# A linear-attention and gated feed-forward kernel: how the stores of the later pairs' x are cut into rows

## The chip, the cores and the metric

The kernel runs on one core of one Trainium2 chip. The metric is device time in microseconds (us) of one execution. A core has a matrix engine (TensorE, PE in the rows; PEld is its loading of weights), a vector engine (VectorE, DVE), a scalar engine (ScalarE, ACT), GpSimd (POOL) and SyncE (SP), which issues nearly all DMAs here. The profile counts 16 DMA engines.

## What is computed

Sizes: 8 batches, 8 heads, 576 positions, 64 features a head; phi maps 64 features to 128 and takes both signs, 256 in all. The attention's output is x, 4,608 tokens of 512 features, and goes through a gated feed-forward net.

```python
def phi(x):
    proj = np.einsum('bhsd,df->bhsf', x, w_phi)
    proj = proj - np.max(np.abs(proj), axis=-1, keepdims=True)
    return np.concatenate([np.exp(proj), np.exp(-proj)], axis=-1)
q_p, k_p = (phi(q), phi(k))
kv = np.einsum('bhsf,bhsd->bhfd', k_p, v)
z = np.sum(k_p, axis=2)
num = np.einsum('bhsf,bhfd->bhsd', q_p, kv)
den = np.einsum('bhsf,bhf->bhs', q_p, z)[..., None] + 1e-06
x = (num / den).transpose(0, 2, 1, 3).reshape(B * S, H * D)
g = x @ w_gate
out = (g / (1 + np.exp(-g)) * (x @ w_val)) @ w_out
```

## The kernel before

The attention works on 32 pairs of heads (8 batches, 4 pairs each). Pairs 0 to 11 take one path (`finish_early`), pairs 12 to 31 another (`finish`); the change is in the second. The feed-forward net takes x in 12 chunks of 384 tokens, with x lying feature by feature (128 rows of features, tokens along the row). The first four chunks are computed plainly; the later eight in pairs of chunks, with sums of operands that save products (`operands`, `strassen`, line 1218). Each such pair of chunks is followed by the second layer (`rest`, line 388, products with `w_hi`, `hh` and the tiles `m`). Weights, their low parts, and the hidden layer pass through DRAM and are streamed in again: `stream_*<-wv_dram` and `tb<-wv_dram` (line 1152), `m<-h_dram` (line 994).

Since x of batches 2 and later is finished long before the net reads it, it goes through DRAM too, in `x_dram`, shaped [batch, 128 rows, 2 halves of the sequence, 4 pairs, 288 positions]. A pair has two heads of 64 features, and so 128 rows. In `finish`, a pair's normalised result lies in `num` with 128 partitions = (head h, half of the sequence u, position s of 32) and, along the row, nine blocks of 64 features. VectorE turns it in blocks of 32 by 32 (line 786): one instruction for each half g of the features, into `turned` with partitions (h, u, feature j of 32) and 288 positions along the row. Two pairs share the tiles (index r). After the second of them SP issues four stores (line 798), one for each h and g: 64 partitions (u, j), each with a row of 2 x 288 float32 numbers, 2,304 bytes. There are 20 such pairs, 10 groups of four stores. `turned` takes the place of `shared`, four tiles that the weights' conversion used earlier, and has two halves n used in turn, each filled again only when the stores of the pair before last are out (`last["sent", ...]`).

Before a pair of chunks is computed, `operands` loads x from `x_dram` into `stage` (line 1166), ACT rounds it into `tb` (line 1176) and VectorE takes the remainder (line 1177).

What is issued when is set by a planner (`Plan`): every step has an engine, a cost in ns and the steps that it waits for, and a run through these costs gives the order of each engine's queue. A transposition costs `dve(n)` = 150 + 1.04 n there, a DMA its bytes at 320 per ns and 2,400 ns. Where TensorE has nothing ready, the planner puts in filler matmuls (`idle`, lines 1415 and 1417). Each engine then works in order; SP's DMAs go round eight completion semaphores, so that each waits for the one eight places before it (the brackets in the order below).

Of the kernel before, what the change touches and what calls it, by code (L numbers as in the profile page):

```python
# [9 lines left out]
F32 = mybir.dt.float32  # L10
F32R = mybir.dt.float32r
U32 = mybir.dt.uint32
# [5 lines left out]
P = 128  # L18
S = 576
SH = S // 2  # L20
NBL = S // 32
D = 64
NF = 128
CH = 384
DM = 512
# [19 lines left out]
LATE_BATCH = 2  # L45
# [32 lines left out]
class Plan:  # L78
# [21 lines left out]
    def add(self, eng, cost, fn, after=(), rank=0.0, take=None, give=None, mode="whole"):  # L100
        port = eng in ("DVE2", "POOL")
        eng = eng[:3] if eng == "DVE2" else eng
        s = Step(eng, cost, fn, rank, len(self.steps), self.LAG[eng], take, give, (rank, len(self.steps)))
        s.port = port
        s.slack = self.SLACK.get(eng, 0) if 16 <= rank < 1000 and cost > 1 else 0
        s.mode = mode if eng == "PE" and cost > 1 else None
        seen = set()
        for a in after:
            if a is not None and id(a) not in seen:
                seen.add(id(a))  # L110
                a.then.append(s)
                s.left += 1
        self.steps.append(s)
        return s
# [146 lines left out]
def dve(n):  # L261
    return 150 + 1.04 * n
# [23 lines left out]
def favor_attention_moe(ctx: ExitStack, tc: tile.TileContext, qT, kT, v, w_phi, wg, wv, wo, out):  # L286
    nc = tc.nc
# [3 lines left out]
    pool = ctx.enter_context(tc.tile_pool(name="sb", bufs=1))  # L291
# [4 lines left out]
    x_dram = tc.dram_tile([NB - LATE_BATCH, P, 2, NK, SH], F32, name="x_dram")  # L296
# [36 lines left out]
    osb = sb("osb", [P, DM], F32, 2)  # L333


    shared = [pool.tile([P, 2 * DM], dt, name=f"shared{i}", tag=f"shared{i}") for i, dt in enumerate((U32, U32, F32, F32))]
    raw = [t.rearrange("p (n t) -> p n t", t=2) for t in shared[:2]]
    we, wa = ([t[:, i * DM:(i + 1) * DM] for i in range(2)] for t in shared[2:])
    late = {}
# [1 line left out]
    def later(name, tag, shape, dtype=F32R):  # L341
        if name not in late:
            late[name] = pool.tile(shape, dtype, name=name, tag=tag)
        return late[name]
# [22 lines left out]
    add = plan.add  # L367
# [111 lines left out]
            at = end  # L479
        return got  # L480

    turned_tiles = []

    def turned_tile(n, g):
        if not turned_tiles:
            turned_tiles.extend(pool.tile([P, 2, SH], F32, name=f"turned{m}", tag=f"shared{m}") for m in range(4))
        return turned_tiles[2 * n + g]

    STAGE_TAGS = ("xh1", "xl1")

# [27 lines left out]
    last = {}  # L518

    def attention(i, rank):  # L520
        b, pr = divmod(i, NPAIR)
        early = i < EARLY_PAIRS
        j = i % 2
        jq = j if early else 0
        vec = nc.vector
# [13 lines left out]
        n = 4 * P * P  # L539
# [11 lines left out]
        for g, (t0, t1) in enumerate(K_GROUPS):  # L551
# [4 lines left out]
            n = m2 * NF  # L556
# [19 lines left out]
            m = km[(3 * i + g) % len(km)]  # L576
# [67 lines left out]
        if early:  # L644
            for g in range(3):
                tail = g == 2
                w = 1 if tail else 4
                n = 3 * i + g
                key, key2 = ("q", i, g), ("t", i, g)
                m, y = km[n % len(km)], qy[n % 2]  # L650
# [103 lines left out]
        def finish(extra):  # L754
            features = lambda k, h, c: (qe, qx)[k][j][:, h, c]
            main, blocks_ = 7, NBL // 2
            slot_at = lambda n: (work[plan.bank["n", i, n // main]], n % main * VD)

            def over():
                for n in range(blocks_):  # L760
                    o, at = slot_at(n)
                    for k in range(2):
                        for h, r in enumerate(sides):
                            nc.tensor.matmul(o[r, at:at + VD], features(k, h, slice(D * n, D * n + D)),  # L764
                                             kvs[j][:, (2 * k + h) * VD:(2 * k + h + 1) * VD],
                                             start=n % main == 0 and k == 0, stop=n in (main - 1, blocks_ - 1) and k == 1)

            nu = add("PE", 2 * blocks_ * KV_PACE, over, [*f1, *kvc, *extra], rank,
                     take=[("n", i, 0), ("n", i, 1)], mode="columns")
            last["kvs", i] = last["nu", i] = last["qe", i] = last["qx", i] = nu  # L770
            parts_ = ((0, 0, main), (1, main, blocks_ - main))
            slots = lambda part, m: work[plan.bank["n", i, part]][:, :m * VD].rearrange("p (n d) -> p n d", d=VD)
            free = [*last.get(("num", i - 1), ()), last.get(("turned", i - 1))]
            dn = [add("ACT", 200, lambda part=part, at=at, m=m: nc.scalar.activation(
                den[:, at:at + m], slots(part, m)[:, :, D], AF.Copy, bias=1e-6), [nu, last.get(("rc", i - 1))], rank)
                for part, at, m in parts_]
            t1 = add("DVE", 200, lambda: vec.reciprocal(rc[:, :blocks_], den[:, :blocks_]), [*dn, *free], rank)
            last["rc", i] = t1
            even = num.rearrange("p (n d) -> p n d", d=D)
            normal = [add("DVE", dve(m * D), lambda part=part, at=at, m=m: vec.tensor_tensor(  # L780
                out=even[:, at:at + m], in0=slots(part, m)[:, :, :D], op=ALU.mult,
                in1=rc[:, at:at + m].rearrange("p (n o) -> p n o", o=1).broadcast_to([P, m, D])), [t1, *free], rank, give=("n", i, part))
                for part, at, m in parts_]
            n, r = i // 2 % 2, i % 2
            over_ = [*raw_free, *wa_free, *we_free] if i < EARLY_PAIRS + 4 else last["sent", i - r - 4]
            t3 = [add("DVE", dve(SH), lambda g=g: vec.transpose(
                turned_tile(n, g)[:, r].rearrange("p (n s) -> p n s", s=32), even[:, :, 32 * g:32 * g + 32]),
                [*normal, *over_], rank) for g in range(2)]
            last["turned", i] = t3[1]
            last["num", i] = t3  # L790
            if r == 0:
                last["half", i] = t3
                return
            t3 = [*t3, *last["half", i - 1]]
            sent = []
            for h in range(2):
                for g in range(2):
                    sent.append(add("SP", D * S * 4, lambda h=h, g=g: nc.sync.dma_start(
                        x_dram[b - LATE_BATCH, (2 * h + g) * 32:(2 * h + g + 1) * 32, :, pr - 1:pr + 1].rearrange("j p r s -> p j (r s)"),
                        turned_tile(n, g)[h * D:(h + 1) * D].rearrange("p r s -> p (r s)")), t3, rank))  # L800
            last["sent", i - 1] = sent
            for c, *_ in cuts:
                x_kept.setdefault(c, []).extend(sent)
# [69 lines left out]
        if early:  # L873
            finish_early([])
        elif i < DEFER:
            finish([])
        else:
            late_sums.append(finish)
# [70 lines left out]
    def first(c, f, low, held):  # L949

        n, lo, lo_ready = low
        a_hi, a_lo = xh[c % X_SETS], xl[c % X_SETS]
        ends = [None, None]
        order = [(a, k) for ks in ((0, 1, 2), (3,)) for a in range(2) for k in ks] if f == 0 else \
            [(a, k) for a in range(2) for k in range(NK)]
        count = [0, 0]
        for a, k in order:
            begin, final = count[a] == 0, count[a] == NK - 1
            count[a] += 1

            def go(a=a, k=k, begin=begin, final=final):
                begun.append(1)
                o = ps(("gv", a, held), CH)
                hi = w1_hi(f)
                matmuls([(o, hi[:, a, k], a_hi[:, k], begin, False), (o, hi[:, a, k], a_lo[:, k], False, False),
                         (o, lo[a][:, k], a_hi[:, k], False, final)])

            wait = list(lo_ready) + (x_ready[c, k] if f == 0 else [])
            if begin:
                wait.append(gv_read[a])  # L970
            ends[a] = product(3 * pe(CH), go, wait)
        lo_user[0][n].append(ends[1])
        if f == NFT - 1:
            x_free[c] = [ends[0], ends[1]]
        j = new_th()

        s1 = into(j, add("ACT", act(CH), lambda: nc.scalar.activation(th(j), ps(("gv", 0, held), CH), AF.Tanh, scale=0.5),
                         [ends[0]], FIRST))
        s2 = add("DVE", dve(CH), lambda: nc.vector.scalar_tensor_tensor(
            out=th(j), in0=th(j), scalar=1.0, in1=ps(("gv", 0, held), CH), op0=ALU.add, op1=ALU.mult), [s1], FIRST)  # L980
        gv_read[0] = s2
        s3 = add("DVE", dve(CH), lambda: nc.vector.tensor_tensor(out=th(j), in0=th(j), in1=ps(("gv", 1, held), CH), op=ALU.mult),
                 [s2, ends[1]], FIRST)
        gv_read[1] = s3
        return j, s3
# [378 lines left out]
    for f in range(NFT):  # L1364
# [3 lines left out]
        for c in range(EARLY):  # L1368
            j, h = first(c, f, low, 0)
# [18 lines left out]
    for f in range(NFT):  # L1388
        j, h = first(PLAIN - 1, f, low_parts(f, 0), 0)
# [80 lines left out]
```

## Time and profile before

| | us |
|---|---|
| median of 3 runs | 1231.64 (1229.57 to 1232.07) |
| the profiled execution | 1231.18 |
| its span, first to last instruction | 1229.4 |
| TensorE busy | 1172.2 (95%) |
| VectorE busy | 793.4 (65%) |
| ScalarE busy | 545.3 (44%) |
| GpSimd busy | 140.9 (11%) |
| mean granted TensorE clock | 0.978 of full speed |

298.32 MB move in 219,744 packets of the queue that SP fills, 243 GB/s as a mean; their time is 75.4% of what 16 DMA engines have. Engines' busy times overlap, so they say nothing yet of what the kernel waits for: that is read from stretches of the span, from the idle time of TensorE in them, and from what ended it. A granted clock of 1.00 is 2.4 GHz, 0.50 is 1.2 GHz.

### The profile page before, as it was taken

To read this page: it belongs to the slowest core of one execution; us is meant where nothing else is said; L and a number is where in the kernel's file an instruction comes from. 1 tells how busy PE (TensorE), PEld (TensorE's weight loads), DVE (VectorE), ACT (ScalarE), POOL (GpSimd) and SP (SyncE) were. 2 spreads that over 40 slices of the span, in tenths; PEclk is the share of its full clock that TensorE was granted. 3 is DMA by queue.
4 is the path that set the end of the run, shared out by engine and by line. 5 is a ranking of instruction groups with operands and counts; after the bars stand their busy time and mean duration, and the time that the engine had idled before them with its cause. 6 is when DMAs were issued, how large, how long until landed. Compare 5 with 4: busy or idle time off the path is not lost. (4 is left out here: it accounts for less than half of the span.)

```text
span 1229.4 us, 26393 instructions
## 1 busy us (share of the span) xinstructions
PE 1172.2 (95%) x9978; PEld 1026.6 (84%) x9978; DVE 793.4 (65%) x1593; ACT 545.3 (44%) x1233; POOL 140.9 (11%) x142
## 2 busy tenths in 40 slices
PE   9999999999999889998979899997999999799998
PEld 7777889999888768987967789896699897599986
DVE  7998899997567637676756255785345785434441
ACT  6887543333435435453534243553333553333332
POOL 1323200000132212010100001110001110001100
PEclk9999999999999989998989899998999999899999
DMA  5656778777999779986766688866688767779864
GB/s 162 175 162 186 247 249 288 249 254 234 333 310 303 253 253 339 344 240 201 242 189 184 198 283 285 241 211 212 221 270 286 238 213 221 244 233 309 281 200 160
DMA packets 220031, 298.32 MB, mean 243 GB/s; under 512 B 65280, under 2 KB 125824, under 8 KB 219904
## 3 DMA queue, kind: packets, MB, share of 16 engines
q1 hardware_dynamic: 219744, 296.56, 75.4%
q8 instruction: 79, 1.29, 0.5%
q14 instruction: 48, 0.39, 0.1%
q10 hardware_dynamic: 160, 0.07, 0.0%
HBM read 217.91 MB, written 78.64 MB: 241 GB/s over the span
## 5 line engine op out<-in xcount | busy, mean ns | idle before, releaser
L388 PE MATMUL work<-w_hi,hh 128*128 128x512 f32 x468 | 187.7, 409 | 24.6 <-ACT hh L1006 16.7
L381 DVE TENSOR_TENSOR m<-m,hh 128x384 fp32r<-128x384 f32 x132 | 74.8, 573 | 140.1 <-ACT hh L1006 122.1
L388 PE MATMUL work<-w_hi,m 128*128 128x512 f32 x396 | 160.6, 405 | 0.9 <-DVE m L381 0.9
L1240 DVE TENSOR_TENSOR m<-m,work 128x384 f32<-128x384 f32 x144 | 78.5, 552 | 121.9 <-ACT m L1237 73.2
L1006 ACT CAST hh<-m 128x384 fp32r<-128x384 f32 x144 | 73.1, 512 | 182.8 <-DMA m<-h_dram 92.3
L381 POOL TENSOR_TENSOR m<-m,m 128x384 f32<-128x384 f32 x48 | 58.4, 1216 | 646.3 <-DVE m L1245 365.3
L388 PE MATMUL work<-xh,w_big 128*128 128x384 f32 x384 | 132.3, 345 | 0.0
L388 PEld LDWEIGHTS work<-w_hi,hh 128*128 128x128 f32 x468 | 90.4, 193 | 48.0 <-ACT hh L1006 18.6
L388 PE MATMUL work<-xl,w_big 128*128 128x384 f32 x384 | 128.6, 335 | 0.0
L1218 PE MATMUL work<-tb,stream_xh 128*128 128x384 f32 x618 | 115.3, 338 | 0.0
L1218 PEld LDWEIGHTS work<-tb,stream_xh 128*128 128x128 f32 x618 | 107.0, 188 | 4.7 <-issue 3.8
L1237 ACT COPY m<-work 128x384 f32<-128x384 f32 x144 | 68.1, 474 | 79.2 <-PE work L1218 71.5
L1218 PE MATMUL work<-tb,stream_xl 128*128 128x384 f32 x468 | 90.8, 343 | 9.1 <-ACT m L1237 9.1
L1244 ACT ACTIVATE m<-m 128x384 f32<-128x384 f32 x96 | 45.4, 517 | 111.4 <-DVE m L1240 111.3
L388 PEld LDWEIGHTS work<-w_hi,m 128*128 128x128 f32 x396 | 76.5, 193 | 20.5 <-DVE m L381 2.4
L1218 PEld LDWEIGHTS work<-tb,stream_xl 128*128 128x128 f32 x468 | 82.7, 191 | 12.7 <-ACT m L1237 9.5
L588 ACT ACTIVATE kp<-kp 128x512 f32<-128x512 f32 x128 | 78.2, 630 | 24.4 <-DVE kp L583 23.2
L1218 PE MATMUL work<-tb,tb 128*128 128x384 f32 x408 | 79.3, 341 | 4.6 <-ACT m L1237 4.6
L388 PEld LDWEIGHTS work<-xh,w_big 128*128 128x128 f32 x384 | 72.2, 188 | 7.7 <-issue 4.8
L1218 PEld LDWEIGHTS work<-tb,tb 128*128 128x128 f32 x408 | 71.8, 191 | 7.5 <-ACT m L1237 4.9
L381 POOL TENSOR_TENSOR s<-s 128x256 f32<-128x256 f32 x48 | 43.1, 897 | 282.4 <-DMA s<-w_dram 250.4
L388 PE MATMUL work<-w_lo,hh 128*128 128x512 f32 x183 | 74.1, 405 | 0.0
(141 smaller groups left out, 2345.8 us busy)
## 6 DMA issues: line engine op xcount, KB each, us to landing
stream_xh<-wv_dram SPq DMA_DIRECT2D x103, 256.0 KB
h_dram<-m SPq DMA_DIRECT2D x124, 192.0 KB
m<-h_dram SPq DMA_DIRECT2D x124, 192.0 KB
stream_xl<-wv_dram SPq DMA_DIRECT2D x78, 256.0 KB
tb<-wv_dram SPq DMA_DIRECT2D x77, 256.0 KB
w_lo<-wlo_dram SPq DMA_DIRECT2D x72, 256.0 KB
stream_w_lo<-wv_dram SPq DMA_DIRECT2D x52, 256.0 KB
stream_xl<-wlo_dram SPq DMA_DIRECT2D x48, 256.0 KB
```

What stands on the lines that cost most here:

```text
L381: (nc.gpsimd if on == "POOL" else nc.vector).tensor_tensor(out=o, in0=a, in1=b, op=op)
L388: nc.tensor.matmul(o, l, r, start=a, stop=z)
L588: nc.scalar.activation(kpv[:, :m2, s], kpv[:, :m2, 1], AF.Exp, scale=-1.0 if s else 1.0)
L1006: s4 = add("ACT", act(CH), lambda: nc.scalar.copy(hh[b], th(j)), [made, hid_free[b]], FIRST)
L1218: nc.tensor.matmul(o(), l, r, start=begin and k + m == 0, stop=k + m == 3, skip_group_check=True)
L1237: return j, into(j, add("ACT", act(CH), lambda: nc.scalar.copy(th(j), src()), after, FIRST))
L1240: return add("DVE", dve(CH), lambda: vec.tensor_tensor(out=th(j), in0=th(j), in1=src(), op=ALU.add), after, FIRST)
L1244: s1 = into(t, add("ACT", act(CH), lambda: nc.scalar.activation(th(t), th(j), AF.Tanh, scale=0.5), [ready], FIRST))
```

## The change

One tile `shared` of 4 x 1,024 numbers a row takes the place of four; `turned` becomes one tile [128, n, g, r, 288] in its place. A pair is turned by one VectorE instruction for both halves of the features instead of two. The four stores of two pairs are cut by head h and half of the sequence p instead of by h and g: each takes 32 partitions (feature j), and from each of them two rows of 2,304 bytes, one for each g. The outermost dimension, on both sides, is 32 where it was 2 in DRAM and 64 in SBUF. Bytes, the number of stores and the length of the rows stay.

```diff
-    shared = [pool.tile([P, 2 * DM], dt, name=f"shared{i}", tag=f"shared{i}") for i, dt in enumerate((U32, U32, F32, F32))]
+    shared = pool.tile([P, 4, 2 * DM], F32, name="shared", tag="shared")
+    shared = [shared[:, i].bitcast(dt) for i, dt in enumerate((U32, U32, F32, F32))]
...
-    turned_tiles = []
-
-    def turned_tile(n, g):
-        if not turned_tiles:
-            turned_tiles.extend(pool.tile([P, 2, SH], F32, name=f"turned{m}", tag=f"shared{m}") for m in range(4))
-        return turned_tiles[2 * n + g]
+    turned = lambda n: later("turned", "shared", [P, 2, 2, 2, SH], F32)[:, n]
...
-            t3 = [add("DVE", dve(SH), lambda g=g: vec.transpose(
-                turned_tile(n, g)[:, r].rearrange("p (n s) -> p n s", s=32), even[:, :, 32 * g:32 * g + 32]),
-                [*normal, *over_], rank) for g in range(2)]
-            last["turned", i] = t3[1]
+            t3 = [add("DVE", dve(S), lambda: vec.transpose(
+                turned(n)[:, :, r].rearrange("p g (n s) -> p n g s", s=32), even.rearrange("p n (g s) -> p n g s", g=2)),
+                [*normal, *over_], rank)]
+            last["turned", i] = t3[0]
...
             for h in range(2):
-                for g in range(2):
-                    sent.append(add("SP", D * S * 4, lambda h=h, g=g: nc.sync.dma_start(
-                        x_dram[b - LATE_BATCH, (2 * h + g) * 32:(2 * h + g + 1) * 32, :, pr - 1:pr + 1].rearrange("j p r s -> p j (r s)"),
-                        turned_tile(n, g)[h * D:(h + 1) * D].rearrange("p r s -> p (r s)")), t3, rank))
+                for p in range(2):
+                    sent.append(add("SP", D * S * 4, lambda h=h, p=p: nc.sync.dma_start(
+                        x_dram[b - LATE_BATCH, h * D:(h + 1) * D, p, pr - 1:pr + 1].rearrange("(g j) r s -> j g (r s)", g=2),
+                        turned(n)[(2 * h + p) * 32:(2 * h + p + 1) * 32].rearrange("p g r s -> p g (r s)")), t3, rank))
```

The planner's cost for a pair's transposition falls from 2 x 449.5 to 749 ns, and with it some of the order moves. Line numbers after the change are 4 lower behind the stores. First SP's queue about its first group of stores (`wv_dram<-s`, `s<-w_dram`: sums of weights; `vf`, `vl`, `kin`, `qin`: inputs of a pair; brackets: what it waits for), before and after:

```order
L1103 DMA wv_dram<-s_3532 128x2x256 [waits DMAHW2_49,Activation_49]
L994 DMA m_4596<-h_dram 128x384 [waits DMAHW3_49]
L989 DMA h_dram<-m_4594 128x384 [waits DMAHW4_49,DVE_49]
L798 DMA x_dram<-turned_4107 2x32x576 [waits DMAHW5_49]
L798 DMA x_dram<-turned_4108 2x32x576 [waits DMAHW6_49,DVE_49]
L798 DMA x_dram<-turned_4107 2x32x576 [waits DMAHW7_49]
L798 DMA x_dram<-turned_4108 2x32x576 [waits DMAHW0_49]
L932 DMA w_lo_89<-wlo_dram 128x512 [waits DMAHW1_49,PE_49]
L1106 DMA wv_dram<-s_3531 128x4x256 [waits DMAHW2_49,DVE_49]
```

```order
L990 DMA m_4361<-h_dram 128x384 [waits DMAHW0_49]
L532 DMA qin<-in_qT_dram 128x576 [waits DMAHW1_49,PE_49]
L794 DMA x_dram<-turned 32x2x576 [waits DMAHW2_49,DVE_49]
L794 DMA x_dram<-turned 32x2x576 [waits DMAHW3_49]
L794 DMA x_dram<-turned 32x2x576 [waits DMAHW4_49]
L794 DMA x_dram<-turned 32x2x576 [waits DMAHW5_49]
L525 DMA kin<-in_kT_dram 128x512 [waits DMAHW6_49,PE_49]
L529 DMA kin<-in_kT_dram 64x2x64 [waits DMAHW7_49,PE_49]
L940 DMA w_lo_85<-wlo_dram 128x512 [waits DMAHW0_49]
```

The group now stands 27 places earlier, ahead of the keys (`kin`) that it followed. Next VectorE where the third late pair is turned (`rc`, `num`: its normalisation), before and after:

```order
L777 RECIPROCAL rc<-den 128x9
L780 TENSOR_TENSOR num<-work_132,rc 128x448
L780 TENSOR_TENSOR num<-work_136,rc 128x128
L786 STREAM_TRANSPOSE turned_4109<-num 128x288
L786 STREAM_TRANSPOSE turned_4110<-num 128x288
L381 TENSOR_TENSOR m_4596<-m_4596,hh_122 128x384
```

```order
L776 TENSOR_TENSOR num<-work_129,rc 128x448
L776 TENSOR_TENSOR num<-work_130,rc 128x128
L782 STREAM_TRANSPOSE turned<-num 128x9x2x32
L382 TENSOR_TENSOR m_4579<-m_4579,hh_122 128x384
L382 TENSOR_TENSOR s_3528<-s_3528 128x256 x2
```

Two instructions became one of twice the length. Last TensorE at the start of the second layer behind the first pair of later chunks, where the number of filler matmuls changes, before and after:

```order
L388 MATMUL work_130<-w_hi_83,m_6777 128x512
L1417 MATMUL work_135<-idle 128x256 x3
L388 MATMUL work_135<-w_hi_84,hh_121 128x512
L388 MATMUL work_135<-stream_xl_5366,hh_121 128x512
L388 MATMUL work_135<-w_hi_84,m_6849 128x512
```

```order
L389 MATMUL work_127<-w_hi_73,hh_122 128x512
L389 MATMUL work_127<-stream_xl_5356,hh_122 128x512
L389 MATMUL work_127<-w_hi_73,m_6797 128x512
L1413 MATMUL work_132<-idle 128x256 x10
L389 MATMUL work_132<-w_hi_74,hh_123 128x512
L389 MATMUL work_132<-stream_xl_5356,hh_123 128x512
```

The three fillers ahead of the second hidden tile became one, and ten stand now ahead of the fourth; over the whole program those of line 1417 (1413 now) go from 60 to 67.

## Rows read from the trace of the kernel before

**Rows 1.** Busy us (instructions) by engine, clock, DMA share, GB/s; nine stretches and all:
```profile
core 0: us, PE busy (x) PEld busy (x) DVE busy (x) ACT busy (x) POOL busy (x), PEclk, DMA share, GB/s
410.70:450.70 40.00, 30.50 (x321) 25.17 (x318) 16.72 (x37) 11.97 (x28) 5.36 (x7) 0.88 0.62 202
...
1038.20:1066.00 27.80, 20.16 (x76) 15.49 (x75) 6.58 (x13) 6.39 (x13) 0.00 (x0) 0.82 0.70 221
sum 264.50, PE 213.99 PEld 176.72 DVE 118.45 ACT 91.13 POOL 12.39; mean PE 23.78 PEld 19.64 DVE 13.16 ACT 10.13 POOL 1.38
...
405.00:1066.00 661.00, 610.49 (x5248) 534.04 (x5245) 388.67 (x813) 278.65 (x627) 59.32 (x48) 0.96 0.76 243
```

**Rows 2.** SP's issues in order of time: start us, us, what:
```profile
430.13 3.54 SPq L798 DMA_DIRECT2D x_dram<-turned  x4
433.78 2.65 SPq L1106 DMA_DIRECT2D wv_dram<-s  x1
```

**Rows 3.** SP's waits from 405 to 1065 us: us, times, longest:
```profile
SPq L1166 <- DMA x_dram<-turned: 16.6, 6, 4.9
SPq L1152 <- DMA x_dram<-turned: 11.4, 8, 2.6
SPq L994 <- DMA x_dram<-turned: 10.9, 7, 2.5
```

**Rows 4.** Two short stretches behind store groups, columns of rows 1:
```profile
434.00:436.00 2.00, 2.00 (x10) 1.59 (x10) 1.15 (x4) 2.00 (x6) 0.00 (x0) 1.00 0.13 51
...
1008.00:1010.00 2.00, 2.00 (x13) 1.75 (x14) 1.59 (x4) 0.91 (x2) 0.00 (x0) 1.00 0.12 42
```

**Rows 5.** Waits from 424 to 430 us, columns of rows 3:
```profile
ACT hh L1006 <- DMA m<-h_dram: 9.3, 1, 9.3
...
PE work L388 <- ACT hh L1006: 4.9, 1, 4.9
```

**Rows 6.** Waits from 627 to 637 us:
```profile
ACT tb L1176 <- DMA stage<-x_dram: 9.6, 2, 9.4
...
PE work L1218 <- ACT m L1237: 9.1, 1, 9.1
```

**Rows 7.** Waits from 1051 to 1061.5 us:
```profile
ACT tb L1176 <- DMA stage<-x_dram: 5.2, 1, 5.2
```

**Rows 8.** The seven stretches at half clock (four shown), columns of rows 1:
```profile
427.06:433.89 6.83, 4.17 (x10) 3.29 (x11) 4.19 (x8) 2.95 (x7) 0.00 (x0) 0.50 0.62 202
447.54:454.37 6.83, 4.96 (x11) 3.64 (x12) 4.05 (x8) 3.35 (x7) 3.30 (x4) 0.50 0.85 272
...
631.86:642.10 10.24, 5.17 (x15) 4.98 (x16) 4.59 (x10) 5.73 (x12) 0.00 (x0) 0.50 0.85 268
...
1055.11:1065.35 10.24, 5.56 (x15) 3.99 (x14) 2.98 (x6) 2.82 (x6) 0.00 (x0) 0.50 0.87 280
sum 54.63, PE 35.23 PEld 29.35 DVE 25.80 ACT 21.67 POOL 4.30; mean PE 5.03 PEld 4.19 DVE 3.69 ACT 3.10 POOL 0.61
```

**Rows 9.** Line 388 alone, 4 us at half and 4 at full clock:
```profile
450.00:454.00 4.00, 4.00 (x10) 2.81 (x9) 3.07 (x7) 2.02 (x5) 1.85 (x2) 0.50 0.99 334
455.00:459.00 4.00, 4.00 (x19) 3.23 (x18) 2.12 (x5) 1.34 (x3) 0.00 (x0) 1.00 1.06 361
```

**Rows 10.** Groups by line and shape, VectorE: busy us, mean ns, idle before:
```profile
L739 DVE STREAM_TRANSPOSE qe<-peaks 128x576 f32<-128x576 f32 x40 | 29.5, 761 | 0.2
...
L786 DVE STREAM_TRANSPOSE turned<-num 128x288 f32<-128x288 f32 x40 | 17.9, 465 | 0.6
```

**Rows 11.** The same view, TensorE's filler matmuls of line 1417:
```profile
L1417 PE MATMUL work<-idle 128*128 128x256 f32 x60 | 10.1, 288 | 0.0
```

**Rows 12.** Three stretches about the first store groups, columns of rows 1:
```profile
405.00:525.00 120.00, 110.50 (x870) 94.96 (x868) 70.86 (x149) 53.51 (x116) 19.01 (x15) 0.94 0.87 294
375.00:390.00 15.00, 15.00 (x208) 12.84 (x207) 9.09 (x23) 7.89 (x20) 4.26 (x6) 1.00 0.98 302
450.00:525.00 75.00, 75.00 (x513) 64.92 (x513) 49.93 (x105) 37.32 (x81) 14.29 (x9) 0.97 0.99 341
```

## The prediction

> **What bounds the kernel now.** I read the busy time by stretches first, because the share over the span (TensorE 95%) hides where it stops. Between 405 and 1066 us TensorE is busy 610.49 of 661 us, so it idles 50.5 us [rows 1]. Then I cut that time into nine stretches, each beginning with the first issue of a group of four stores `x_dram<-turned` and ending some 24 to 40 us later, where TensorE runs again at full clock. There are ten groups, 40 stores; the first stretch holds two groups. The nine together last 264.5 us and TensorE is busy for 213.99 of them: 50.5 us idle. The whole idleness of 661 us lies behind a store group, and none of it in the other 396.5 us.
>
> So I looked at what the queues do there. SP issues four stores in 3.54 us, and the next issue alone takes 2.65 us [rows 2]; SP also waits for these stores to land, 16.6 us before loads of `stage`, 11.4 us before weight loads, 10.9 us before loads of hidden tiles [rows 3]. The instruction order shows why a load of something else waits for them: SP's DMAs go round eight completion semaphores, and each waits for the one eight places before it. Four slow stores hold four of the eight places. And slow they are: where nothing else is left in flight, the DMA engines are 0.13 and 0.12 busy and move 51 and 42 GB/s [rows 4]. 2 of 16 engines are 0.125. A store is 64 rows of 2,304 bytes, so a group of four is 590 KB; at 51 GB/s that is 11.6 us. The other fourteen engines have nothing to do, since SP can't get past. The hidden tile that `ACT hh` needs then comes 9.3 us late and TensorE idles 4.9 us [rows 5].
>
> **The change, part by part.**
>
> (1) *The stores.* Their outermost dimension was 2 (two halves of the sequence), and two engines carried them. It becomes 32, on both sides of the transfer, with the same 64 pieces of 2,304 bytes for each. No row of this trace shows a transfer with 32 rows outermost; the bounds are 51 GB/s, as now [rows 4], and the 341 GB/s that the engines hold over 75 us with wide transfers [rows 12]. I take the upper end, because all else that SP issues has 64 or 128 rows outermost, and the engines' share reaches 0.99 with it [rows 12]: the narrow rate stands only where the 2 stands. A group then takes 590/341 = 1.7 us in place of 11.6, and holds places in the round of eight no longer than any load.
>
> The Trainium skill says the same from the other side (DMA: Bandwidth & Descriptors, "Rules for kernel authors", use all 16 engines): the number of engines is set by the slowest dimension that isn't 1, and one of size c below 16 confines the DMA to c engines. The 0.13 share agrees for 2; that 32 gives 16 is the page's alone, and by it the sum below comes out as I have it.
>
> What it gives back: the idle time, 50.5 us [rows 1], and the clock. After seven of the stalls the granted clock is 0.50 (1.2 GHz) for 54.63 us in all, 35.23 of them busy [rows 8]. At 0.50 ten matmuls of line 388 fall in 4 us, at 1.00 nineteen [rows 9], so a busy microsecond there does 10/19 of the work, and 35.23 x 9/19 = 16.6 us are lost. Together 50.5 + 16.6 = 67.1 us. The clock fell only behind stalls of TensorE, so if they go, it stays up.
>
> (2) *The transposes.* 40 of 128x288 at 465 ns become 20 of 128x576; the nearest row, 128x576 in one piece, is 761 ns [rows 10]. 40 x 0.465 - 20 x 0.761 = 3.4 us less VectorE time in all. VectorE is busy 388.67 of 661 us there [rows 1] and the stores wait for both transposes anyway; I count nothing. Were the scattered destination (18 blocks to two regions) to cost twice as much, 20 x 0.76 = 15 us would be spread over 20 places of a VectorE with 272 us to spare.
>
> (3) *One tile in place of four.* `shared` keeps its bytes; a transposition writes both feature halves of one half of the tile. The waits of the weight pieces are the same ones in the instruction order, and the store still waits for the pair before. Nothing.
>
> (4) *The order.* The planner's costs change by 150 ns a pair, and it moves things: SP's first store group comes 27 places earlier, ahead of two loads of keys; on TensorE, matmuls of projections and of the FFN change places, and the filler matmuls grow from 60 to 67 (three become one, ten new ones stand before the fourth hidden tile's products). 60 cost 10.1 us [rows 11], so 7 cost 1.2 us where they stand on the path. I take 1.2; at the other end 0, as filler in a wait costs nothing.
>
> (5) *What is late next.* With the stalls gone the same bytes must move in less time. From 405 to 525 us the engines move 294 GB/s over 120 us [rows 12], 35.3 MB. TensorE loses there 9.5 us idle and (4.17 + 4.96) x 9/19 = 4.3 us of clock [rows 8], so without stalls 106.2 us are left, 332 GB/s. The engines held 341 from 450 to 525, but only 302 from 375 to 390, at a share of 0.98 [rows 12]. At 341 it fits and nothing comes back; at 302 it takes 116.9 us and 10.7 come back. The average of the rest is well below (a share of 0.76 over 661 us) [rows 1]. I take a third of 10.7, 3.5 us, since the need lies nearer to 341.
>
> Sum, against the profiled execution (1231.18 us, 1229.4 of it the span, 1.8 around it): 1231.2 - 67.1 + 1.2 + 3.5 = 1168.8, so **1169 us**. The median is 1231.64, 0.46 above; that is left in the range. A difference under 0.2% (2.5 us) is about what can't be told from no change.
>
> **The rivals.**
>
> *The x round trip stays.* Some stalls end with `stage<-x_dram`: ACT waits 9.4 us for a staged x and TensorE 9.1 us behind it [rows 6]; the stretch from 1038 us, with 7.64 us idle [rows 1], has 5.2 us of the same kind [rows 7]. If it is the latency of store, load and split that is late, and not the two engines, these 9.1 + 7.6 = 16.7 us stay, and with them two clock falls of 10.24 us each, (5.17 + 5.56) x 9/19 = 5.1 us [rows 8]. Then 1168.8 + 21.8 = 1190.6 us. For it: the chain is long and in-order on ACT. Against it: SP itself waits 16.6 us for these stores before it can issue the stage loads [rows 3], and that is the part that goes. 0.13.
>
> *The store doesn't spread.* The two streams come from something else, the pieces or the destination's rows, and 32 outermost changes nothing: 1231 us. For it: no row shows a 32-row transfer. Against it: all wide transfers run on all engines. 0.04.
>
> *Slower: the store spreads, but 32 rows can't be read faster.* If a store's 32 rows of SBUF gave no more than 51 GB/s together, all sixteen engines would be held for 11.6 us where two are now, ten times. The stretches now move about 200 GB/s (202 in the first, 221 in the last) [rows 1], so some 150 GB/s of other traffic, 17 MB in 116 us, would have to move afterwards, 50 us at 341 GB/s: 1281 us. It decides where a group takes longer than 6.7 us (67.1/10), under 88 GB/s. Against it: the two engines now reach 51 GB/s from 64 rows, 25 each [rows 4], more than the 21 that each of sixteen gives at 341 [rows 12]; nothing there looks like a limit of the rows. 0.03. The Trainium skill speaks against it too (SBUF — State Buffer, "Door 1: The DMA port swizzle"): rows 0 to 31 reach the same 8 of 16 ports as rows 0 to 63, about 218 GB/s, so 2.7 us a group by estimate, and no run here shows it.
>
> *Half comes back.* The moved order, or hidden tiles that were late anyway, keep two fifths to two thirds of the 67.1 us, 27 to 45: 1196 to 1214 us. For it: it is a hidden tile that comes late [rows 5], and not the stores themselves. Against it: the 396.5 us without a store group before them hold no stall at all. 0.08.
>
> **How the numbers follow.** My forecast has 0.72: 1164 (nothing comes back, fillers free) to 1177 (all 10.7 us of (5) come back, and the median's 0.5). The range takes in the round trip at 1190 with a little room, and below it 3 us for small gains: 1161 to 1193. It leaves out the last three rivals and the fringes, about 2 in 10. Faster by over 0.2%: 0.72 + 0.13 + 0.08 = 0.93. Within 0.2%: 0.04. Slower: 0.03.
>
> **What would show it.** Right: behind a store group the DMA share no longer drops to 0.13, GB/s stays above 200; SP's waits for `x_dram<-turned` fall from about 39 us to a few; TensorE's idle time between 405 us and the last store is under 10 us; the granted clock stays at 1.00 for nearly all of the span, 0.99 or more as a mean. Round trip: the DMA share holds, but `ACT tb` still waits for `stage<-x_dram`. No spread: 42 to 51 GB/s behind the stores as before. Rows as limit: the share is high behind a store, but GB/s low. Wrong altogether would be a trace in which the share holds and TensorE still idles behind the groups: then the stores only stood where another wait falls.

## The result, and the profile after

The changed kernel takes 1163.06 us (median of 4 runs, 1161.04 to 1163.23) where the kernel before took 1230.61 in the same session (4 runs, 1227.02 to 1232.07): 0.945 of the time, with an interval of 0.943 to 0.948. The profiled execution is the shortest of the four, 1161.04 us with a span of 1159.2. Of one kernel below, that with 24+8 rows, one run took 1401.45 us at a granted clock of 0.753 and is left out there.

Three lines of the page of the kernel after: busy time by engine, the granted clock and the DMA share in 40 slices.

```profile
PE 1152.4 (99%) x9985; PEld 1015.2 (88%) x9985; DVE 793.7 (68%) x1573; ACT 546.7 (47%) x1233; POOL 139.6 (12%) x142
...
PEclk9999999999999999999999999999999999999999
...
DMA  5546678777799999997887788887888787889774
```

TensorE idles 1159.2 - 1152.4 = 6.8 us of the whole span, and no slice has a lowered clock. The stretches that answer to [rows 1], [rows 4] and [rows 12], with the same columns. The first is all the time in which stores are issued (they start at 389.7 and end at 981.4 us); then come three short pieces behind groups of stores, and two long ones in which the engines have most to move:

```profile
385.00:1010.00 625.00, 624.56 (x5477) 550.25 (x5476) 419.21 (x862) 298.80 (x670) 64.48 (x56) 1.00 0.85 272
...
393.00:395.00 2.00, 2.00 (x12) 1.86 (x11) 1.25 (x5) 1.40 (x4) 0.00 (x0) 1.00 0.86 271
427.00:429.00 2.00, 1.91 (x9) 1.25 (x8) 1.05 (x3) 1.40 (x3) 0.00 (x0) 1.00 1.05 383
982.00:984.00 2.00, 2.00 (x11) 1.59 (x10) 0.56 (x1) 0.41 (x2) 0.00 (x0) 1.00 0.93 297
...
385.00:505.00 120.00, 119.91 (x992) 102.62 (x991) 86.59 (x182) 59.88 (x133) 22.91 (x22) 1.00 0.97 332
430.00:505.00 75.00, 75.00 (x566) 64.59 (x566) 46.97 (x98) 35.57 (x79) 13.37 (x10) 1.00 1.00 346
```

Of 625 us TensorE idles 0.44, where 50.5 of 661 were idle [rows 1]. Behind the groups the DMA share is 0.86 to 1.05 where it was 0.13 and 0.12 [rows 4]. TensorE has one wait left in that time. SP has none for `x_dram<-turned` that is listed, where [rows 3] had 39 us; its longest are now for TensorE, which is to say that loads are ahead of their use. Both answers, TensorE's waits and the head of SP's, with the columns of [rows 3]:

```profile
PE work L1214 <- ACT m L1233: 0.4, 1, 0.4
```

```profile
SPq L1148 <- PE work L1214: 105.0, 181, 1.8
SPq L1148 <- PE work L389: 64.7, 47, 4.0
SPq L538 <- PE work L594: 28.8, 14, 3.2
```

The tile `turned` itself, answering to [rows 2] and [rows 10] (count: shortest, median and longest in ns, first and last start in us):

```profile
L794 SPq DMA_DIRECT2D x_dram<-turned x40: 318/427/1211, 389.7 to 981.4; - x40
L782 DVE STREAM_TRANSPOSE turned<-num x20: 768/778/780, 365.8 to 976.8; 128x576 f32<-128x576 f32 x20
...
DMA to landing us min/median/max: 2.2/3.6/5.3
```

A store lands 3.6 us after its issue, like the loads around it: in the page's part on DMA issues (count, KB each, median us to landing) a hidden tile takes 4.1.

```profile
m<-h_dram SPq DMA_DIRECT2D x124, 192.0 KB, 4.1
```

**Where the 70.2 us of the span went.** The kernel before was busy on TensorE for 1172.2 us of its 1229.4 (page of the kernel before), so it idled 57.2. Idle time fell by 57.2 - 6.8 = 50.4 us, busy time by 1172.2 - 1152.4 = 19.8, and the two make the whole difference.

### The profile page after: what moved, and what is told of

Same layout as the page of the kernel before. It is cut to its first block, busy times and chain, and to the rows that moved or that the text cites. A ratio compares the mean times of both kernels' runs of the same rounds, so it can differ in the third digit from the quotient of the medians.

```text
span 1159.2 us, 26379 instructions
## 1 busy us (share of the span) xinstructions
PE 1152.4 (99%) x9985; PEld 1015.2 (88%) x9985; DVE 793.7 (68%) x1573; ACT 546.7 (47%) x1233; POOL 139.6 (12%) x142
## 4 chain that ended last, share of the span: by engine, by line
PE 86%; DVE 1%; DMA 1%; issue 0%; SPq 0%; ACT 0%; ACTq 0%
PE work L389 41%; PE work L1214 31%; PE work L760 4%; PE work L601 4%; PE work L705 2%; PE work L562 2%; PE work L594 1%; PE work L1413 1%; DMA w_lo<-wlo_dram 0%; DMA stage<-x_dram 0%; PE work L565 0%; PE work L817 0%; PE work L813 0%; PE work L677 0%; DVE qy L667 0%
## 5 line engine op out<-in xcount | busy, mean ns | idle before, releaser
L389 PE MATMUL work<-w_hi,hh 128*128 128x512 f32 x468 | 183.1, 399 | 0.0
L1236 DVE TENSOR_TENSOR m<-m,work 128x384 f32<-128x384 f32 x144 | 78.6, 552 | 117.7 <-ACT m L1233 67.8
L389 PE MATMUL work<-w_hi,m 128*128 128x512 f32 x396 | 156.7, 396 | 0.0
L389 PEld LDWEIGHTS work<-w_hi,hh 128*128 128x128 f32 x468 | 87.9, 188 | 21.5 <-issue 1.7
L584 ACT ACTIVATE kp<-kp 128x512 f32<-128x512 f32 x128 | 78.5, 630 | 26.5 <-DVE kp L579 25.3
L601 PEld LDWEIGHTS work<-vf,kp 128*64 128x64 f32 x2048 | 62.6, 138 | 13.4 <-issue 5.5
L389 PEld LDWEIGHTS work<-xl,w_big 128*128 128x128 f32 x384 | 72.2, 188 | 1.0
```

The source lines that it names most:

```text
L389: nc.tensor.matmul(o, l, r, start=a, stop=z)
L584: nc.scalar.activation(kpv[:, :m2, s], kpv[:, :m2, 1], AF.Exp, scale=-1.0 if s else 1.0)
L601: nc.tensor.matmul(ps_kv()[r, (2 * s + h) * VD:(2 * s + h + 1) * VD], kpv[:, t, s, r], vf[:, t, h], start=t == 0 and h + s == 0, stop=False)
L1236: return add("DVE", dve(CH), lambda: vec.tensor_tensor(out=th(j), in0=th(j), in1=src(), op=ALU.add), after, FIRST)
```

## The experiments

All edits are to the changed kernel, in the stores unless told otherwise. Each was timed against the kernel before on its chip, and ratios are to that.

**Which part of the change does it?** Two kernels undo one half each. The first has the stores cut as before and all else as after, its order too:

```diff
-                for p in range(2):
+                for g in range(2):
...
-                        x_dram[b - LATE_BATCH, h * D:(h + 1) * D, p, pr - 1:pr + 1].rearrange("(g j) r s -> j g (r s)", g=2),
-                        turned(n)[(2 * h + p) * 32:(2 * h + p + 1) * 32].rearrange("p g r s -> p g (r s)")), t3, rank))
+                        x_dram[b - LATE_BATCH, (2 * h + g) * 32:(2 * h + g + 1) * 32, :, pr - 1:pr + 1].rearrange("j p r s -> p j (r s)"),
+                        turned(n)[h * D:(h + 1) * D, g].rearrange("p r s -> p (r s)")), t3, rank))
```

> The kernel after, with the stores alone cut as before (by head and half of the features, two halves of the sequence outermost, 64 rows); tile, transposes and the order of every engine stay those of after. Theory (two engines carry a store whose outermost dimension is 2): the stalls return, 1222 to 1240 us, DMA share near 0.13 and some 50 GB/s behind a store group, half clock again for 40 us or more. Rival (the new order or the single transposes gave the gain): 1160 to 1175 us. Rival (both share): about 1195 us.

Measured: 1233.3 us (1231.23 to 1235.78), 1.0039 of the kernel before [1.0024, 1.0054]. All of the gain is gone. Its page and two short pieces behind store groups:

```profile
PE 1172.7 (95%) x9985; PEld 1026.5 (83%) x9985; DVE 792.3 (64%) x1573; ACT 545.3 (44%) x1233; POOL 139.0 (11%) x142
```

```profile
436.00:438.00 2.00, 0.00 (x0) 0.00 (x0) 0.40 (x2) 0.57 (x1) 0.00 (x0) 1.00 0.14 47
1010.00:1012.00 2.00, 2.00 (x13) 1.79 (x11) 1.71 (x4) 0.69 (x2) 0.00 (x0) 1.00 0.17 50
```

The share of two engines and some 50 GB/s are back, and TensorE, with the same 9,985 matmuls as after, is busy 1172.7 - 1152.4 = 20.3 us longer. The second kernel keeps the new stores and the one tile and turns each pair in two pieces; with that it has the order of the kernel before:

```diff
-            t3 = [add("DVE", dve(S), lambda: vec.transpose(
+            t3 = [add("DVE", dve(SH), lambda g=g: vec.transpose(
...
+                [*normal, *over_], rank) for g in range(2)]
```

> The kernel after, with two transposes a pair as before, each at the planner's old cost, so that every engine has the order of before; the stores have 32 rows outermost. Theory (the stores alone give the gain): 1160 to 1168 us; VectorE about 2.4 us busier than after (40 x 0.465 in place of 20 x 0.777), TensorE's idle time between 405 us and the last store group under 5 us. Rival (the new order is needed): 1175 us or more, with stalls where the order differs, from 400 to 450 us above all.

Measured: 1161.11 us (1160.83 to 1162.26), 0.9442 [0.9417, 0.9466]. So the four corners are 1228.9 (old order, old stores, median of that session), 1161.1 (old order, new stores), 1233.3 (new order, old stores) and 1163.1 (both new). The cut of the stores is worth 67.8 us in the old order and 70.2 in the new one (there against the 1163.1 of the first session); the new order and the single transposition are worth nothing that can be told beside the new stores, and lose 0.4% beside the old ones.

**How does the changed cut act?** Theory: a store with 32 rows outermost is carried by all sixteen DMA engines, one with 2 by two; as the number of engines follows from the outermost size, cuts of the same 32 rows into other sizes must fall and rise with it. The rival: something else in the new cut (its partitions, or its rows in DRAM) is what helps. Each store is cut in two parts of 16+16, 24+8, 25+7 and 31+1 rows; the bytes and pieces stay, and there are 80 stores, each planned by itself, which moves the order. The edit for 31+1; in the others 31 is 16, 24 or 25:

```diff
-                for p in range(2):
+                for p, lo, hi in ((0, 0, 31), (0, 31, 32), (1, 0, 31), (1, 31, 32)):
...
-                        x_dram[b - LATE_BATCH, h * D:(h + 1) * D, p, pr - 1:pr + 1].rearrange("(g j) r s -> j g (r s)", g=2),
-                        turned(n)[(2 * h + p) * 32:(2 * h + p + 1) * 32].rearrange("p g r s -> p g (r s)")), t3, rank))
+                        x_dram[b - LATE_BATCH, h * D:(h + 1) * D, p, pr - 1:pr + 1].rearrange("(g j) r s -> j g (r s)", g=2)[lo:hi],
+                        turned(n)[(2 * h + p) * 32 + lo:(2 * h + p) * 32 + hi].rearrange("p g r s -> p g (r s)")), t3, rank))
```

> The kernel after, each store cut into two stores of 16 and 16 rows (80 in all, the same rows and bytes). 16 rows over 16 engines: four pieces of 2,304 bytes a group on each engine for each head and half, 16 pieces x 93 ns = 1.5 us a group. Both theories: 1160 to 1172 us, the upper end for 40 more issues on SP of 0.4 us each and a moved order.

> As k16, but cut into 24 and 8 rows, planner's costs and order those of k16. Theory of the Trainium skill (DMA: Bandwidth & Descriptors, how many engines: the largest number up to 16 that divides the outermost sizes): 8 engines each, 32 pieces on a busy engine, 3.0 us a group; within 0.5% of k16. Rival (engines are filled in turn whatever the size): the same time, so this run is for the dose between 16 and 1.

> As k16, but cut into 25 and 7 rows. By the page 5 and 7 engines: 4 x (10 + 2) = 48 pieces on the five busiest, 4.5 us a group against 11.9 for two engines. The prefetch covered some 14 us from a first store to the first stall in the kernel before, so: within 1% of k16, stalls of under 10 us in all. Rival (stalls grow in proportion to the time that the busiest engine is held): (4.5 - 1.5) / (11.9 - 1.5) x 70 = 20 us over k16.

> As k16, but cut into 31 and 1 rows. By the page one engine carries all: 256 pieces x 93 ns = 23.8 us a group, 12 us more than in the kernel before. Theory: slower than the kernel before, 1300 to 1380 us, with a DMA share near 0.06 and 25 GB/s behind the stores. Rival (31 rows go to 16 engines, two rows each and one left over, or the number of engines isn't set by divisors): as k16.

Measured: 16+16 rows 1164.82 us (1162.7 to 1165.15), 0.9466 [0.9452, 0.9481]; 24+8 rows 1163.54 (three runs, 1160.93 to 1163.88), 0.9453 [0.9435, 0.9472]; 25+7 rows 1162.91 (1161.89 to 1166.42), 0.9452 [0.9436, 0.9467]; 31+1 rows 1312.62 (1310.62 to 1313.1), 1.0668 [1.0652, 1.0684]. Twice the issues cost nothing, and neither do 24 or 25 rows; 31 rows cost 148 us against 16, with the same partitions, the same rows in DRAM and the same bytes. Behind its groups the kernel with 31+1 shows, where that with 25+7 shows the third line:

```profile
448.00:450.00 2.00, 2.00 (x10) 1.62 (x9) 1.63 (x4) 1.42 (x3) 0.00 (x0) 1.00 0.07 25
450.00:452.00 2.00, 2.00 (x11) 1.59 (x10) 0.56 (x1) 1.47 (x4) 0.00 (x0) 1.00 0.06 25
```

```profile
401.00:403.00 2.00, 2.00 (x11) 1.64 (x9) 2.00 (x5) 0.53 (x1) 1.04 (x2) 1.00 0.98 354
```

One sixteenth is 0.0625, and 25 GB/s is half of the 51 in [rows 4]: one engine where there were two. The rival falls. The Trainium skill (DMA: Bandwidth & Descriptors, "Why a DMA increments its semaphore by 16 and not by 1") has the rule: a DMA goes to the largest number of engines, 16 at most, that divides the outermost sizes of both sides, where a size of 1 is passed over. By it 2 rows go to two engines and 31, a prime, to one, and both traces agree.

The traces also count the engines, in the semaphore events by which each DMA tells that it has landed. In the kernel before each of the 40 stores has three such events and every other DMA sixteen; of a store's three, one comes soon after the issue and two at the end. Counted over all stores of a kind, 31 rows give 2 events, 17 rows 2, 25 rows 6, 7 rows 8, 24 rows 13, 8 rows 9, and 16 or 32 rows 16. Below sixteen that is one more than the engines by the rule: 1, 1, 5, 7, 12 and 8. The expectation for 24+8 put 24 rows on 8 engines; the rule gives 12 and the trace agrees, so that cut holds an engine for less long than was expected.

**How long may an engine be held?** Where some of a group's eight stores have 17 rows, again a prime, and the rest 15 or 16, one engine is held for a part of the time that 31 rows take. The edit for one head; for both, m is 17 throughout:

```diff
+                m = 17 if h == 0 else 16
+                for p, lo, hi in ((0, 0, m), (0, m, 32), (1, 0, m), (1, m, 32)):
```

> As k16 (80 stores, its order), but the stores of one head of each pair are cut into 17 and 15 rows, those of the other into 16 and 16. 17 is prime, so by the page one engine carries the 17 rows: 2 x (34 + 2) + 8 = 80 pieces on it a group, 80 x 93 ns = 7.4 us, against 1.5 in k16, 11.9 in the kernel before and 23.8 in k1. Theory (what the loads ahead cover is free, and only the rest stalls TensorE; k5 with 4.5 us cost nothing): 1163 to 1175 us. Rival (time grows in proportion to how long the busiest engine is held, as from k16 to k1, 148 us for 22.3): 1165 + 39 = 1204 us.

> As one_half, but for both heads: 144 pieces a group on one engine, 13.4 us, near the 11.9 us of two engines in the kernel before, with half the bytes of a group on the other engines. Theory (it counts how long the busiest engine is held, not how many engines there are): 1225 to 1260 us. Rival (a single held engine among 16 does half the harm of two): 1190 to 1210 us.

Measured: with one head 1181.83 us (1180.42 to 1183.72), 0.9617 [0.9601, 0.9633]; both heads 1213.82 (1212.37 to 1215.34), 0.9872 [0.9856, 0.9888]. Each lies between its two expectations, and so confirms neither. These kernels and those above with two parts have one order, so they make a series. The hold of the busiest engine for one group is an estimate: the rows that the rule gives it in the eight stores, each of 2 x 2,304 bytes, over the 25 GB/s that one engine moved.

| cut | most rows on one engine, in eight stores | hold, us (estimate) | time, us | over 16+16 |
|---|---|---|---|---|
| 16+16 | 8 | 1.5 | 1164.8 | |
| 24+8 | 12 | 2.2 | 1163.5 | -1.3 |
| 25+7 | 24 | 4.4 | 1162.9 | -1.9 |
| one head 17+15 | 40 | 7.4 | 1181.8 | +17.0 |
| both heads 17+15 | 72 | 13.3 | 1213.8 | +49.0 |
| 31+1 | 126 | 23.2 | 1312.6 | +147.8 |

A hold of 4.4 us cost nothing and one of 7.4 did; from there the ten groups pass on a growing part: 1.7 us each at 7.4, 4.9 at 13.3, 14.8 at 23.2. That it is the lead of the loads over their use that covers the short holds fits this and was not measured apart.

**Is it the held engines or the queue behind them?** The prediction said that the other fourteen engines had nothing to do because SP could not get past (theory A: the round of eight semaphores). The rival (theory B): SP gets past, but every wide load has pieces on the held engines too, and these come behind the stores' pieces. First the narrow stores were issued by ACT, so that SP's own stream has no stores, and with them the wide stores as a control, whose edit is shown (the other has the same change of issuer on the stores cut by h and g):

```diff
-                    sent.append(add("SP", D * S * 4, lambda h=h, p=p: nc.sync.dma_start(
+                    sent.append(add("SP", D * S * 4, lambda h=h, p=p: nc.scalar.dma_start(
```

> As narrow, but the four stores of a group are issued by ACT and not by SP, at the same place of the plan. Theory A (SP's round of eight completion semaphores is what the slow stores block): SP goes on, DMA share behind a store group stays above 0.4, 1163 to 1185 us. Theory B (every other transfer has a piece on the two engines that are held, and waits behind 11.6 us of stores there): stalls stay, 1200 us or more, though SP no longer waits for these stores. If ACT itself is held while it issues, its gaps show at the stores' line.

> Control for act_narrow: the stores of after (32 rows outermost), issued by ACT. Four issues of 0.4 us a group, 16 us of ACT in all on an engine that is busy 47%: both theories 1160 to 1168 us. Anything slower is the price of issuing on ACT and is taken off act_narrow.

Measured: narrow from ACT 1244.1 us (1243.15 to 1248.18), 1.012 [1.0093, 1.0147]; wide from ACT 1162.88 (1161.66 to 1163.45), 0.9452 [0.9431, 0.9473]. The control shows that it doesn't matter who issues a wide store. The other was meant to part the theories and doesn't: the instruction order shows that ACT's DMAs take their places in the same round of eight, and SP waits for the stores no less. SP's waits in it, and the stores' issues on ACT:

```profile
SPq L990 <- DMA x_dram<-turned: 30.9, 8, 8.7
...
SPq L1148 <- DMA x_dram<-turned: 24.2, 7, 4.4
SPq L1162 <- DMA x_dram<-turned: 20.2, 4, 8.0
```

```profile
L794 ACTq DMA_DIRECT2D x_dram<-turned x40: 500/503/4589, 389.1 to 1052.9; - x40
```

So the round was filled more: eight narrow stores a group, each with rows of half the length, on two engines, in the order of 16+16:

```diff
+                for g, k in ((0, 0), (0, 1), (1, 0), (1, 1)):
...
+                        x_dram[b - LATE_BATCH, (2 * h + g) * 32:(2 * h + g + 1) * 32, :, pr - 1 + k].rearrange("j p s -> p j s"),
+                        turned(n)[h * D:(h + 1) * D, g, k]), t3, rank))
```

> Two engines as in the kernel before, but eight stores a group, one for each head, half of the features and pair, rows of 1,152 bytes; order and number of stores those of k16. 512 pieces x 51 ns / 2 engines = 13.1 us a group. All eight places of the round of completion semaphores are held by stores, not four. Theory A (the round is what stops SP): worse than narrow by more than the 1.2 us a group of smaller pieces, 1255 us or more. Theory B (any transfer with a piece on a held engine is late, whether SP could issue it or not): 1230 to 1250 us.

Measured: 1208.28 us (1206.01 to 1213.16), 0.9832 [0.9807, 0.9857]. That is a miss for both theories: 25 us faster than four narrow stores, though eight places of the round go to the stores of a group and not four. They don't hold all eight at once: other DMAs stand between them, and in the first group the fifth store was issued at 404.86 us, when the first had landed (403.56). What it and the kernel with both heads at 17+15 (1213.8) share is the order of 16+16, in which the stores of a group are planned one by one. The last kernel keeps the 17+15 rows and takes that away: two issues in one planned step, so that the order is that of the changed kernel.

```diff
...
+                    def both(h=h, p=p):
+                        for lo, hi in ((0, 17), (17, 32)):
+                            nc.sync.dma_start(
+                                x_dram[b - LATE_BATCH, h * D:(h + 1) * D, p, pr - 1:pr + 1].rearrange("(g j) r s -> j g (r s)", g=2)[lo:hi],
+                                turned(n)[(2 * h + p) * 32 + lo:(2 * h + p) * 32 + hi].rearrange("p g r s -> p g (r s)"))
+                    sent.append(add("SP", D * S * 4, both, t3, rank))
```

> As one_17 (one engine carries the 17 rows of each store, 13.4 us a group), but in the order of after: each of the four stores of a group is issued as two in a row, 17 and 15 rows, where after has one. It lies beside narrow (two engines, 11.9 us a group, the same order, 1233 us) and one_17 (one engine, 13.4 us, 1214 us, the stores of a group planned as eight and spread among other transfers). If the order makes the difference: 1230 to 1255 us, narrow's time and up to 1.5 us a group more. If one held engine does less harm than two: 1205 to 1222 us, as in one_17.

Measured: 1236.13 us (1235.4 to 1238.59), 1.0054 [1.0036, 1.0072]. The same parts cost 22.3 us more in this order. SP's issues at the first group, with both heads at 17+15 in the order of 16+16 and then in that of the changed kernel (start us, us, what, how many):

```profile
395.93 0.39 SPq L795 DMA_DIRECT2D x_dram<-turned  x1
396.37 0.40 SPq L991 DMA_DIRECT2D m<-h_dram  x1
396.82 1.35 SPq L795 DMA_DIRECT2D x_dram<-turned  x1
398.26 0.66 SPq L1103 DMA_DIRECT2D wv_dram<-s  x1
398.96 2.13 SPq L795 DMA_DIRECT2D x_dram<-turned  x2
401.19 0.99 SPq L941 DMA_DIRECT2D w_lo1g<-wlo_dram  x1
402.29 0.70 SPq L941 DMA_DIRECT2D w_lo1v<-wlo_dram  x1
403.04 0.49 SPq L795 DMA_DIRECT2D x_dram<-turned  x1
403.62 0.39 SPq L986 DMA_DIRECT2D h_dram<-m  x1
404.07 4.65 SPq L795 DMA_DIRECT2D x_dram<-turned  x3
```

```profile
390.78 6.73 SPq L796 DMA_DIRECT2D x_dram<-turned  x8
397.60 0.36 SPq L525 DMA_DIRECT2D kin<-in_kT_dram  x1
398.06 1.07 SPq L529 DMA_DIRECT2D kin<-in_kT_dram  x1
```

Spread over 13 us with five other issues between them, or eight in a row. The two orders differ at other places too, so the 22.3 us belong to the order as a whole. With it set, one engine and two make little difference: 1236.1 (one) beside 1233.3 (two) in one order, 1213.8 beside 1208.3 in the other. From the first issue of a group to the last landing of its stores, by the semaphore events, the first pair takes 17.1 and 16.8 us and the second 21.1 and 20.8 (medians of ten groups), so like is compared with like. As far as these two pairs tell, it is the length of the hold that costs, not how many engines are held. Eight stores in a row also fill the round, and cost 2.8 us more than four: that speaks against the number of places as what sets the price, and is what B expects.

Two more readings bear on A and B. SP's waits for stores don't rank the kernels. The largest ones of the kernel with both heads at 17+15 (1213.8 us), and then of that with four narrow stores (1233.3):

```profile
SPq L795 <- DMA x_dram<-turned: 26.5, 12, 3.2
...
SPq L1149 <- DMA x_dram<-turned: 17.1, 8, 2.6
SPq L991 <- DMA x_dram<-turned: 12.7, 7, 2.7
SPq L1163 <- DMA x_dram<-turned: 7.6, 3, 2.6
```

```profile
SPq L1162 <- DMA x_dram<-turned: 15.3, 5, 4.9
SPq L1148 <- DMA x_dram<-turned: 12.5, 7, 2.8
...
SPq L990 <- DMA x_dram<-turned: 8.0, 5, 2.5
```

These rows add up to 63.9 us in the faster kernel, 26.5 of them stores that wait for stores, and to 35.8 in the slower one. And in the kernel before, a load that had been issued landed late: SP's issue of two hidden tiles, and ACT's use of them, with its idle time in brackets.

```profile
437.49 3.78 SPq L994 DMA_DIRECT2D m<-h_dram  x2
```

```profile
448.85 1.01 ACT L1006 CAST hh<-m 128x384 fp32r<-128x384 f32 x2 [12.22 <-DMA m<-h_dram]
```

The issues ended at 441.27, so ACT waited at least 7.6 us more for tiles that SP had got past, where the changed kernel's land in 4.1. The semaphore events show what came late. Of the sixteen events of each tile fourteen were there at 443.53 and 444.00 us; the last two came at 447.99 and 448.77 for the one, 448.49 and 449.27 for the other, behind the last of the group's stores (445.67). Every wide DMA that SP issued from 414 to 430 us, behind the group before, shows such a gap before its last two events (7.4 us at first, 0.5 at the end), and two is the number of engines that carry a store. So B is shown.

A is there too. ACT's wait of 9.64 us for a hidden tile, which ended at 842.03 us, was for a load that landed 4.75 us after its issue, nearly as in the changed kernel; it was issued only at 837.26, after SP had waited for a store that landed at 836.17. How the 67 us divide between the two stays open: the number of places in the round was not changed in any run.

## Why the prediction held, step by step

**Step (1), the stores, is right**, in its size and its place: the 32 rows run on all engines, TensorE's idle time and the lowered clock are gone together, and undoing this part alone undoes everything. The idle term, 50.5, came out at 50.4. The busy time was **mis-sized**: the clock term gave it 16.6 (the product is 16.7), and it fell by 19.8 though 0.5 us of fillers were added, so 20.3; the pair of kernels with the same matmuls gives 20.3 as well. That is 3.7 us more, and not because stretches at half clock were left out: the clock's records of the kernel before, which run from 7.2 us to the end of the span, have the seven and no others before its last 0.2 us. Set against the mean of its shape in the changed kernel, the matmuls in the seven cost about 17.4 us more (an estimate from the two traces), near the term; some 3 us lie outside them, 0.8 of that before the records begin and the rest where the full clock was granted, and their cause stays open.

**The reason given in step (1) is only part of it.** "The other fourteen engines have nothing to do, since SP can't get past" is one of two causes: loads that SP had issued were done on fourteen engines and stood waiting for their pieces on the held two, and eight stores in a row cost hardly more than four. The number was safe from this, since both causes go when the hold goes.

**Step (2), the transposition, is right** about its price to the time, nothing (1161.1 with two, 1163.1 with one). One takes 777 ns, not the 761 of the nearest row [rows 10]: the scattered destination cost next to nothing, and 40 x 0.465 - 20 x 0.777 = 3.1 us come off VectorE's work, which did not need them.

**Step (3)** shows no wait of its own. **Step (4)** was put at 1.2 us; the fillers grew from 10.1 us [rows 11] to

```profile
L1413 PE MATMUL work<-idle 128*128 128x256 f32 x67 | 10.6, 282 | 0.0
```

and so by 0.5. The moved store group is worth nothing beside wide stores.

**Step (5) is the term that failed in kind**: 3.5 us were to come back for want of bandwidth. The stretch of 120 us runs at 332 GB/s, just the need that the prediction worked out, with a DMA share of 0.97 and TensorE idle for 0.09 us. The lower row it weighed, 302 GB/s at a share of 0.98, was no limit for this stretch, nor for the 75 us at 346 in it.

So the sum missed by 3.5 (step 5), 3.7 (busy time beyond the clock term) and 0.7 (fillers), 7.9 us in one direction, against the 7.8 between 1168.8 and the profiled 1161.0; the median is 2.0 above that and was forecast 5.9 too high, inside the range.

**The rivals.** That the x round trip stays: of the staged tiles eight came late, by 7.4 us together, and TensorE had no wait behind them but the 0.4 us shown. That the store doesn't spread, or that its 32 rows can't be read faster: a share of 0.86 to 1.05 at 271 to 383 GB/s speaks against both. That half comes back: nothing did.

## What to carry to other kernels

A store or load whose outermost size gives few DMA engines looks harmless by its bytes, but holds those engines, and the wide transfers behind it were complete here only when their pieces there were: look for short stretches where the DMA share sits at a sixteenth or two, and see what was issued just before. Choose the cut so that the outermost size on both sides is a multiple of 16; where that can't be, keep the hold short (4.4 us cost nothing here, 7.4 did), and try another order of issue: one that spread the narrow stores among other issues was 22 us faster, though what in it did that is not shown. And test the cut apart from the order that comes with it, since the order moved by itself here was worth nothing, or a little less.

## What the runs showed of the hardware beyond that

- Behind narrow transfers single issues stand long in the queue, so that not only the engines are held. With 31 rows on one engine, three stores took SP 6.69 us to issue and the transfer of a hidden tile among them 4.62, where 0.3 to 0.6 us is usual; ACT, as issuer of narrow stores, stood up to 4.59 us in one (above):

```profile
407.23 0.31 SPq L794 DMA_DIRECT2D x_dram<-turned  x1
407.67 4.62 SPq L985 DMA_DIRECT2D h_dram<-m  x1
412.34 6.69 SPq L794 DMA_DIRECT2D x_dram<-turned  x3
```

- One held engine of sixteen cost as much as two held for about the same time (1236.1 and 1233.3 us; 1213.8 and 1208.3).
- Eighty issues in place of forty, each half as large, cost nothing that can be told (1164.8 beside 1163.1 us).
